# Masked attention and a gated convolution feed-forward on one core: the value product in two runs of six matmuls, and other places for the copies out of PSUM

## The chip, the cores and the metric

The kernel runs on one core of one Trainium2 chip. A core has a matrix engine (TensorE, PE in the profile, with its weight loads on a row of their own, PEld), VectorE (DVE), ScalarE (ACT), GpSimd (POOL) and SyncE (SP), which here issues nearly all DMAs. Each engine works through its own queue in the order of the program, and waits on semaphores where it needs another engine's result. TensorE writes only to PSUM, a small memory of eight banks, and VectorE or ScalarE must copy the results out. The metric is device time in microseconds of one execution.

## The reference, cut to what matters

```python
# q, k, v: (4, 8, 768, 64); proj: (64, 6)
q_bits = einsum(q, proj) > 0;  k_bits = einsum(k, proj) > 0      # six bits per row
mask   = bucket(q_bits)[:, None] == bucket(k_bits)[None, :]
scores = where(mask, q @ k.T / 8, -1e9)
attn   = exp(scores - max);  attn = attn / (sum(attn) + 1e-9)
x      = (attn @ v), heads side by side                           # (4, 768, 512)
gate   = sigmoid(causal 5-tap convolution of x, channel by channel)
out    = (gate * (x @ w_val)) @ w_out                             # (4, 768, 512)
```

## The kernel before, in words

There are 32 **units**, one for each batch and head. A unit has 768 queries, in six **tiles** of 128. A main loop goes over the 192 tiles of all units, and a pass `k` of it is called a **slot** here. The order of the work is written out by hand: the instructions stand on every engine in the order in which the Python code issues them, and generators (`moes`, `convs`, `preps`, `weights`, `ahead`, `avs`) are stepped at fixed places of a slot, each step issuing a piece of the work that lies beside attention.

Attention for tile `k` passes through several slots:

- `scores(k + 1)` (L266) issues the next tile's scores on TensorE: four matmuls into a PSUM tile `s`, of which there are two. So the scores of a tile need the buffer that the exponential of two tiles before has read.
- `maxima`, `factors`, `shifts` (L272 to L282) run on VectorE, then `exponentials` (L290) on ScalarE, with the row's sum from the accumulator. `row_sums` and `recip` run for two tiles at once, `normalise` (L305) on POOL.
- `transposes(k - 3)` (L314) turns the probabilities on TensorE, six 128 x 128 transposes into two PSUM tiles `tp`, of which there are two.
- `keep_transposed` (L323) copies both to `pt` in SBUF on ScalarE, at the start of the following slot. After a unit's last tile it appends the unit's value product to `avs`.
- `attn_v` (L337) is the value product: for each of six blocks of keys two matmuls, one for each half of the queries, which write the two halves of the partitions of one PSUM tile `av`. For the first three blocks both `pt` read are the first of their pair, for the others the second. The first half of the queries is tiles 0 to 2, the second is tiles 3 to 5. Every odd slot steps it twice, so that a unit's product comes as three **value runs** of four matmuls. After the last, two ScalarE copies (L345) take `av` to `x`.

A unit pair's `x` goes through `pair_x` (casts, five convolution taps, and after a batch's last pair the sigmoids), which appends the batch's feed-forward to `moes`. This consists of **chunks** of twelve matmuls into a PSUM tile of `ps_m`, which has one buffer: eight value chunks (`val`, 384 columns, L399) and six output chunks (`outp`, 512 columns, L424). A step of `moes` issues a third of a chunk, four matmuls. Behind the last, VectorE multiplies with the gate (L404), or ScalarE (VectorE near the gates) copies the output (L430, L432), which a DMA stores. `thin` leaves out the step in odd or even slots around the end of a batch. The last two output chunks of a batch wait in `hold` for the next batch's chunks, and then a whole chunk is issued in each of two slots. The last batch's feed-forward follows behind the loop.

In the first batch no chunk exists yet. Its slots share VectorE, ScalarE and POOL with the preparation of the weights, and carry the bit products (`bits` L204, `early_bits` L226), whose results VectorE marks (L207, L229).

## Time and profile before

| | us |
|---|---|
| runs: median, lowest, highest of 3 | 622.48, 621.9, 624.69 |
| profiled execution, first to last instruction (its span) | 620.8 |
| TensorE busy | 585.5 |
| VectorE busy | 437.6 |
| ScalarE busy | 421.4 |
| GpSimd busy | 395.6 |

The profiled execution's own time is its span, and the median of the runs lies 1.7 us above it. A row of a group or of the timeline names line, engine, operation, the tiles written and read and a count; numbers behind a bar are busy time and mean length, and then the idle time of the engine ahead of these instructions, with what ended it. A row of the busy times by stretch has the stretch, then for PE, PEld, DVE, ACT and POOL the busy time and the number of instructions, then TensorE's granted clock, the DMA share and GB/s. A matmul's length in the trace is modelled and overlaps the next one's, so what a block costs is read from its start to the next block's start.

### The profile page before, as it was taken

The page shows a single profiled execution, that of the slowest core. Times are in us where ns is not written, and L with a number is a line of the kernel's source. Part 1 is how long each engine was busy: PE and PEld are TensorE (multiplying, and loading weights), DVE is VectorE, ACT ScalarE, POOL GpSimd, SP SyncE. Part 2 cuts the span into 40 slices and gives each one's busy share as a digit, 9 for nine tenths or more (in the row PEclk, how much of TensorE's full clock was granted, in tenths as well). Part 3 has the DMA queues.
Part 4 walks back from the last instruction along what each step waited for, and adds up shares of the span by engine and source line. Part 5 has one row for each costly group of instructions (what it writes and reads, how often), then busy time and mean ns, then how long its engine had stood idle before and what let it go on. Part 6 is the DMA issues. An engine that isn't in the chain of part 4 may idle for free.

```text
span 620.8 us, 10648 instructions
## 1 busy us (share of the span) xinstructions
PE 585.5 (94%) x3496; PEld 423.4 (68%) x3496; DVE 437.6 (70%) x1017; ACT 421.4 (68%) x881; POOL 395.6 (64%) x373
## 2 busy tenths in 40 slices
PE   5789898989999999999999999999999999999997
PEld 2655565555657777776767777777667877775895
DVE  5869798998975866668575867569665877665532
ACT  2777777778778666777787676777787766765400
POOL 3576868778766765578564777568764777544321
PEclk9799999999999999999999999999999999999999
DMA  6467666564532235243433234333422213200111
GB/s 227 123 197 199 200 167 208 157 175 118 133 83 68 70 79 142 72 108 82 122 82 107 61 80 126 84 115 82 108 70 78 67 42 91 69 18 1 51 52 51
DMA packets 29031, 64.64 MB, mean 104 GB/s; under 512 B 4937, under 2 KB 10057, under 8 KB 28977
## 3 DMA queue, kind: packets, MB, share of 16 engines
q1 hardware_dynamic: 28832, 63.93, 37.8%
q8 instruction: 28, 0.46, 0.3%
q14 instruction: 27, 0.21, 0.1%
q10 hardware_dynamic: 144, 0.03, 0.0%
HBM read 30.60 MB, written 7.86 MB: 62 GB/s over the span
## 4 chain that ended last, share of the span: by engine, by line
PE 66%; DVE 12%; ACT 12%; DMA 5%; issue 3%; POOL 2%; SPq 1%; ACTq 0%; POOLq 0%; DVEq 0%
PE av L337 17%; PE s L266 16%; PE tp L314 12%; PE m L424 8%; PE m L399 7%; ACT p L290 5%; DVE nm L272 4%; ACT pt L323 3%; ACT x L345 2%; DMA w<-in_w_val_dram 2%; DVE g L368 2%; PE tp L399 1%; PE tp L424 1%; PE s L424 1%; DMA bk<-bq 1%
## 5 line engine op out<-in xcount | busy, mean ns | idle before, releaser
L305 POOL TENSOR_SCALAR p<-p,ri 128x768 f32<-128x768 f32 x192 | 210.5, 1100 | 156.0 <-DVE nb L282 130.8
L272 DVE TENSOR_REDUCE nm<-s 128x1 f32<-128x768 f32 x192 | 182.5, 950 | 61.2 <-PE s L266 61.0
L290 ACT ACTIVATE p<-s,nb,gs 128x768 f32<-128x768 f32 x192 | 192.6, 1003 | 46.2 <-DVE nb L282 41.9
L323 ACT COPY pt<-tp 128x384 f32<-128x384 f32 x384 | 165.7, 485 | 75.3 <-PE tp L314 74.4
L314 PEld LDWEIGHTS tp<-ident,p 128*128 128x128 f32 x1152 | 130.3, 142 | 72.2 <-issue 43.6
L314 PE MATMUL tp<-ident,p 128*128 128x128 f32 x1152 | 164.4, 279 | 2.6 <-ACT pt L323 2.1
L337 PE MATMUL av<-pt,vt 128*64 128x384 f32 x768 | 144.9, 498 | 0.0
L266 PE MATMUL s<-ak,aq 76*128 76x384 f32 x384 | 118.1, 389 | 23.2 <-ACT p L290 19.7
L266 PE MATMUL s<-bk,bq 128*128 128x384 f32 x384 | 101.3, 345 | 0.4 <-DVE bq L252 0.4
L337 PEld LDWEIGHTS av<-pt,vt 128*64 128x64 f32 x768 | 47.0, 136 | 61.5 <-issue 61.4
L266 PEld LDWEIGHTS s<-ak,aq 76*128 76x128 f32 x384 | 59.2, 194 | 38.7 <-ACT p L290 34.6
L368 DVE SCALAR_TENSOR_TENSOR g<-x,cw_sb,g 128x768 f32<-128x768 f32 x64 | 79.4, 1241 | 2.2 <-POOL g L366 2.1
L266 PEld LDWEIGHTS s<-bk,bq 128*128 128x128 f32 x384 | 71.7, 194 | 0.8 <-issue 0.8
L173 POOL TENSOR_TENSOR bq<-r,aq 128x768 fp32r<-128x768 f32 x31 | 59.2, 1909 | 0.1
L410 POOL TENSOR_TENSOR hl<-ht,hh 128x384 fp32r<-128x384 f32 x32 | 32.3, 1009 | 39.5 <-DVE hh L408 39.5
L345 ACT COPY x<-av 64x384 f32<-64x384 f32 x64 | 30.4, 475 | 29.7 <-PE av L337 29.0
L282 DVE TENSOR_SCALAR nb<-nm,gs 128x1 f32<-128x1 f32 x192 | 40.4, 211 | 3.5
L399 PE MATMUL m<-xh,wv 128*128 128x384 f32 x200 | 42.7, 337 | 0.0
L358 POOL TENSOR_TENSOR xl<-x,xh 128x384 fp32r<-128x384 f32 x32 | 33.4, 1059 | 13.8 <-DVE xh L357 13.8
L290 ACT ACTIVATION_READ_ACCUMULATOR p<-s,nb,gs 128x1 f32 x192 | 39.0, 203 | 0.0
L404 DVE TENSOR_TENSOR ht<-m,g 128x384 f32<-128x384 f32 x25 | 13.9, 556 | 35.6 <-PE m L399 29.2
L424 PE MATMUL m<-wo,hh 128*128 128x512 f32 x144 | 38.1, 394 | 0.0
(86 smaller groups left out, 486.9 us busy)
## 6 DMA issues: line engine op xcount, KB each, us to landing
r<-in_qk_dram SPq DMA_DIRECT2D x32, 384.0 KB
vt<-in_v_dram SPq DMA_DIRECT2D x16, 384.0 KB
out_dram<-o SPq DMA_DIRECT2D x24, 256.0 KB
ak<-aq SPq DMA_DIRECT2D x31, 192.0 KB
bk<-aq SPq DMA_DIRECT2D x31, 192.0 KB
bk<-bq SPq DMA_DIRECT2D x31, 192.0 KB
bq<-aq SPq DMA_DIRECT2D x31, 192.0 KB
hh<-in_qk_dram SPq DMA_DIRECT2D x16, 192.0 KB
```

What stands on the lines that cost most here:

```text
L173: nc.gpsimd.tensor_tensor(out=bq, in0=r, in1=aq.bitcast(FP32), op=ALU.subtract)
L266: nc.tensor.matmul(out=s[:, hf, 0:HS], lhsT=lq[0:n, qs], rhs=rk[0:n, hf * HS:(hf + 1) * HS], start=n == M, stop=n == P)
L272: nc.vector.tensor_reduce(out=nm, in_=s[:, :, 0:HS], axis=AX.XY, op=ALU.max, negate=True)
L290: nc.scalar.activation(out=p, in_=s[:, :, 0:HS], func=AF.Exp, bias=nb, scale=gs.pop(k), accum_out=sm[:, k % 2, 0:1])
L305: nc.gpsimd.tensor_scalar(out=p, in0=p, scalar1=rcs.pop(k), scalar2=1.0, op0=ALU.mult, op1=ALU.mult)
L314: nc.tensor.transpose(out=tp[:, n * P:(n + 1) * P], in_=p[:, kb * P:(kb + 1) * P], identity=ident)
L323: nc.scalar.copy(out=pt[:, :, qo:qo + P], in_=tp[:, 0:HS].rearrange("p (a b) -> p a b", b=P))
L337: nc.tensor.matmul(out=av[s * D:(s + 1) * D, 0:HS], lhsT=vt[:, kb, hh * D:(hh + 1) * D], rhs=pt[kb // 3][:, kb % 3, :], start=(kb == 0), s ...
L345: nc.scalar.copy(out=x[hh * D:(hh + 1) * D, o:o + HS], in_=av[s * D:(s + 1) * D, 0:HS])
L368: nc.vector.scalar_tensor_tensor(out=g, in0=x[:, k:k + S], scalar=w, in1=g, op0=ALU.mult, op1=ALU.add)
L399: nc.tensor.matmul(out=acc[:, 0:HS], lhsT=wv[wi][:, c, j * P:(j + 1) * P], rhs=xs_[(c, o)][xi], start=(m == 0), stop=(m == 11))
L424: nc.tensor.matmul(out=acc, lhsT=hs[(o, j)][hi][:, tb * P:(tb + 1) * P], rhs=wo[wi][:, j, :], start=(m == 0), stop=(m == 11))
```

## The change

- `attn_v` is stepped three times in every slot with `k % 3 == 2`, instead of twice in every odd one: two value runs of six matmuls for a unit. They stand behind the transposes, not ahead of them.
- `keep_transposed(k - 3)` follows `transposes(k - 3)` in its own slot. So a unit's value product begins in the slot in which its last tile is transposed (its *first run*; the *second run* comes three slots later).
- A step of `moes` issues half a chunk, six matmuls. It is called in two slots of three (`(1, 1, 0)[k % 3]`), not in every slot with thinner stretches; behind the gates twice in a slot instead of three times.
- What reads a PSUM tile of `av`, of a chunk or of the bits is put into a list, `readers`. The list is emptied by `read()`, which stands behind the exponential of a slot, and at the next request for an accumulator.
- `early_bits` steps at `k % 6` of 1 and 4 instead of 2 and 4, and the loop has one slot less.

```diff
@@ early_bits, bits @@
-            nc.vector.tensor_scalar(out=u[:, sl], in0=z[:, 0:HS], ...)
+            def mark(z=z, sl=sl):
+                nc.vector.tensor_scalar(out=u[:, sl], in0=z[:, 0:HS], ...)
+            soon(mark)
@@ attn_v @@
-        for s in range(2):
-            o = KW - 1 + s * HS
-            nc.scalar.copy(out=x[hh * D:(hh + 1) * D, o:o + HS], in_=av[s * D:(s + 1) * D, 0:HS])
...
+        def take():
...
+            for s in range(2):
+                o = KW - 1 + s * HS
+                nc.scalar.copy(out=x[hh * D:(hh + 1) * D, o:o + HS], in_=av[s * D:(s + 1) * D, 0:HS])
...
+        soon(take)
+
+    def soon(f):
+        readers.append(f)
+        if cur["end"]:
+            read()
+
+    def read():
+        while readers:
+            readers.pop(0)()
@@ acc_tile (and side_tile, prep) @@
+        read()
@@ val (outp alike, with store for gate) @@
-                if m:
-                    yield
                 for c in range(NP):
+                    if m == 6:
+                        later()
+                        yield
...
-            nc.vector.tensor_tensor(out=ht, in0=acc[:, 0:HS], in1=g[j][:, o:o + HS], op=ALU.mult)
+            def gate():
+                nc.vector.tensor_tensor(out=ht, in0=acc[:, 0:HS], in1=g[j][:, o:o + HS], op=ALU.mult)
+                todo.append(split)
...
+            soon(gate)
@@ main loop @@
-        for k in range(N + LAG + 1):
-            if 0 <= k - LAG - 1:
-                keep_transposed(k - LAG - 1)
+        for k in range(N + LAG):
...
                 exponentials(k)
+            read()
...
-            thin = k // 6 % 8 in (7, 0) and k < 186
-            for _ in range(3 if cur["gates"] else (1, 0)[k % 2] if thin else 1):
+            for _ in range(2 if cur["gates"] else (1, 1, 0)[k % 3]):
                 step(moes)
...
-            if 6 <= k < 60 and k % 6 in (2, 4):
+            if 6 <= k < 60 and k % 6 in (1, 4):
                 step(ahead)
-            if k % 2:
-                step(avs)
-                step(avs)
             if 0 <= k - LAG < N:
                 transposes(k - LAG)
+                keep_transposed(k - LAG)
+            if k % 3 == 2:
+                for _ in range(KB // 2):
+                    step(avs)
```

TensorE's queue before, in a slot with a value run between value chunks. `x2` and `x4` count instructions; `Activation` and `Pool` are the semaphores of ScalarE and POOL.

```order
L266 MATMUL s<-ak,aq 128x384 [waits Activation_49]
L266 MATMUL s<-ak,aq 128x384
L266 MATMUL s<-bk,bq 128x384 x2
L399 MATMUL m<-xl,wv_120 128x384 x4
L337 MATMUL av<-pt,vt 64x384 x4
L314 MATMUL tp<-ident,p 128x128 [waits Activation_49,Pool_49]
L314 MATMUL tp<-ident,p 128x128 x2
L314 MATMUL tp<-ident,p 128x128 [waits Activation_49]
L314 MATMUL tp<-ident,p 128x128 x2
```

The run stands ahead of the slot's transposes and this one waits for nothing. TensorE's queue after, in a slot with a unit's first run (scores are L274 now, transposes L322, the value product L345):

```order
L274 MATMUL s<-ak,aq 128x384 [waits Activation_49]
L274 MATMUL s<-ak,aq 128x384
L274 MATMUL s<-bk,bq 128x384 x2
L322 MATMUL tp<-ident,p 128x128 [waits Activation_49,Pool_49]
L322 MATMUL tp<-ident,p 128x128 x2
L322 MATMUL tp<-ident,p 128x128 [waits Activation_49]
L322 MATMUL tp<-ident,p 128x128 x2
L345 MATMUL av<-pt,vt 64x384
L345 MATMUL av<-pt,vt 64x384 [waits Activation_49]
L345 MATMUL av<-pt,vt 64x384 x4
```

The run has moved behind the transposes, no chunk stands in the slot, and the run's second matmul waits for ScalarE.

ScalarE's queue before, around a unit's copies of `av` to `x` (L345; L290 is the exponential, L323 the copies of transposes):

```order
L323 COPY pt<-tp 128x3x128 [waits PE_49,Activation_49]
L290 ACTIVATE p,sm<-s,nb,gs 128x768 [waits DVE_49,Pool_49]
L345 COPY x<-av 64x384 [waits PE_49]
L345 COPY x<-av 64x384
L323 COPY pt<-tp 128x3x128 [waits PE_49] x2
L290 ACTIVATE p,sm<-s,nb,gs 128x768 [waits DVE_49,Pool_49]
```

The copies of `av` stand ahead of the transposes' copies and of the next exponential. ScalarE's queue after, in two slots, the second with a first run and the store of an output chunk (L460; L298 is the exponential, L331 the copies of transposes):

```order
L298 ACTIVATE p,sm<-s,nb,gs 128x768 [waits DVE_49,Pool_49]
L331 COPY pt<-tp 128x3x128 [waits PE_49] x2
L298 ACTIVATE p,sm<-s,nb,gs 128x768 [waits DVE_49,Pool_49]
L460 COPY o<-m 128x512 [waits DMAHW7_49,DMAHW3_49]
L331 COPY pt<-tp 128x3x128 [waits PE_49] x2
```

Readers such as the store now follow the exponential, and the copies of the slot's own transposes come after both. A unit's copies of `av` take the place that the store has here, in the slot behind the unit's second run.

More of the change, by code (lines that the diff above doesn't have):

```diff
@@ L206, in bits @@
                                  tile_position=(0, 32 * jj))
-            nc.vector.tensor_scalar(out=u[:, sl], in0=z[:, 0:HS], scalar1=rows_sb[:, 0:1], scalar2=rows_sb[:, 1:2],
-                                    op0=ALU.is_ge, op1=ALU.mult)
+            def mark(z=z, sl=sl):
+                nc.vector.tensor_scalar(out=u[:, sl], in0=z[:, 0:HS], scalar1=rows_sb[:, 0:1], scalar2=rows_sb[:, 1:2],
+                                        op0=ALU.is_ge, op1=ALU.mult)
+            soon(mark)
         cur["u"] = u
@@ L223, in early_bits @@
                 yield
-                z = ps_m.tile([P, 512], FP32, name="m")
+                z = acc_tile()
                 for jj, t in enumerate(rows[hf]):
@@ L227, in early_bits, with keep @@
                                      tile_position=(0, 32 * jj))
-                t = hp.tile([P, HS], FP32, name="ht", bufs=2)
-                nc.vector.tensor_scalar(out=t.bitcast(FP32R), in0=z[:, 0:HS], scalar1=rows_sb[:, 0:1],
-                                        scalar2=rows_sb[:, 1:2], op0=ALU.is_ge, op1=ALU.mult)
-                nc.sync.dma_start(out=u[:, hf * HS:(hf + 1) * HS], in_=t)
+                def keep(z=z, u=u, hf=hf):
+                    t = hp.tile([P, HS], FP32, name="ht", bufs=2)
+                    nc.vector.tensor_scalar(out=t.bitcast(FP32R), in0=z[:, 0:HS], scalar1=rows_sb[:, 0:1],
+                                            scalar2=rows_sb[:, 1:2], op0=ALU.is_ge, op1=ALU.mult)
+                    nc.sync.dma_start(out=u[:, hf * HS:(hf + 1) * HS], in_=t)
+                soon(keep)
             early[i] = u
@@ L338, in attn_v @@
                                  start=(kb == 0), stop=(kb == KB - 1), tile_position=(0, s * D))
-        if hh == 0:
-            x = cur["x"] = xp.tile([P, S + KW - 1], FP32, name="x")
-            nc.gpsimd.memset(x[:, 0:KW - 1], 0.0)
-        x = cur["x"]
-        for s in range(2):
-            o = KW - 1 + s * HS
-            nc.scalar.copy(out=x[hh * D:(hh + 1) * D, o:o + HS], in_=av[s * D:(s + 1) * D, 0:HS])
-        if hh == 1:
-            if c == 0:
-                cur["xs"], cur["g"] = {}, []
-            convs.append(pair_x(b, c, x, cur["g"], cur["xs"]))
+        def take():
+            if hh == 0:
+                x = cur["x"] = xp.tile([P, S + KW - 1], FP32, name="x")
+                nc.gpsimd.memset(x[:, 0:KW - 1], 0.0)
+            x = cur["x"]
+            for s in range(2):
+                o = KW - 1 + s * HS
+                nc.scalar.copy(out=x[hh * D:(hh + 1) * D, o:o + HS], in_=av[s * D:(s + 1) * D, 0:HS])
+            if hh == 1:
+                if c == 0:
+                    cur["xs"], cur["g"] = {}, []
+                convs.append(pair_x(b, c, x, cur["g"], cur["xs"]))
+        soon(take)
[6 more added lines that the diff above has]
+            readers.pop(0)()
     def pair_x(b, c, x, gs, xs_):
@@ L376, in acc_tile @@
     def acc_tile():
+        read()
         pools = accs
@@ L401, in val @@
                     m += 1
-                later()
+            later()
             ht = hp.tile([P, HS], FP32, name="ht", bufs=2)
-            nc.vector.tensor_tensor(out=ht, in0=acc[:, 0:HS], in1=g[j][:, o:o + HS], op=ALU.mult)
+            def gate():
+                nc.vector.tensor_tensor(out=ht, in0=acc[:, 0:HS], in1=g[j][:, o:o + HS], op=ALU.mult)
+                todo.append(split)
             def split():
@@ L411, in split @@
                 hs[(o, j)] = (hh, hl)
-            todo.append(split)
+            soon(gate)
             yield
@@ L420, in outp @@
             for hi, wi in ((0, 0), (0, 1), (1, 0)):
-                if m:
-                    yield
                 for j in range(NP):
+                    if m == 6:
+                        later()
+                        yield
                     nc.tensor.matmul(out=acc, lhsT=hs[(o, j)][hi][:, tb * P:(tb + 1) * P],
@@ L426, in outp, with store @@
                     m += 1
-                later()
-            ob = op.tile([P, 512], FP32, name="o")
-            if cur["gates"]:
-                nc.vector.tensor_copy(out=ob, in_=acc)
-            else:
-                nc.scalar.copy(out=ob, in_=acc)
-            r0 = o + tb * P
-            nc.sync.dma_start(out=out[b, r0:r0 + P, :], in_=ob)
+            later()
+            def store():
+                ob = op.tile([P, 512], FP32, name="o")
+                if cur["gates"]:
+                    nc.vector.tensor_copy(out=ob, in_=acc)
+                else:
+                    nc.scalar.copy(out=ob, in_=acc)
+                r0 = o + tb * P
+                nc.sync.dma_start(out=out[b, r0:r0 + P, :], in_=ob)
+            soon(store)
             yield
@@ L512 @@
                 exponentials(k)
+            read()
             if k >= 60 or k % 2:
@@ L523 @@
             step(preps)
-            if 6 <= k < 60 and k % 6 in (2, 4):
+            if 6 <= k < 60 and k % 6 in (1, 4):
                 step(ahead)
-            if k % 2:
-                step(avs)
-                step(avs)
             if 0 <= k - LAG < N:
                 transposes(k - LAG)
+                keep_transposed(k - LAG)
+            if k % 3 == 2:
+                for _ in range(KB // 2):
+                    step(avs)
         accs[:] = [(ps_m, "m"), (ps_t, "tp"), (ps_s, "s"), (ps_t, "tp"), (ps_s, "s")]
         finish(avs)
+        read()
         cur["gates"] = 0
```

2 lines of the change are left out of this document (1 added, 1 removed).

## The prediction

> **What bounds the kernel now.** I read the page's first table, then the busy times by stretch, then TensorE's own timeline, where the distance from one start to the next shows what a block of matmuls really takes.
>
> ```profile
> span 620.8 us, 10648 instructions
> PE 585.5 (94%) x3496; PEld 423.4 (68%) x3496; DVE 437.6 (70%) x1017; ACT 421.4 (68%) x881; POOL 395.6 (64%) x373
> 35.00:187.50 152.50, 138.68 (x890) 87.19 (x886) 132.57 (x302) 114.72 (x248) 115.95 (x106) 1.00 0.58 162
> 187.50:331.10 143.60, 140.24 (x841) 104.05 (x841) 96.01 (x234) 108.87 (x225) 95.98 (x91) 1.00 0.36 92
> 331.10:471.70 140.60, 139.15 (x843) 103.85 (x841) 97.51 (x235) 104.09 (x219) 94.30 (x88) 1.00 0.35 92
> L272 DVE TENSOR_REDUCE nm<-s 128x1 f32<-128x768 f32 x56 | 53.1, 949 | 6.2 <-PE s L266 6.2
> ```
>
> The last row is the first stretch's own: 56 maxima in 152.5 us, so 2.72 us a slot, with VectorE busy for 132.57 of them. There VectorE is about as close to its limit as TensorE. From 187.5 on TensorE alone is full. One pair of slots there:
>
> ```profile
> 331.09 0.59 PE L266 MATMUL s<-ak,aq 76*128 76x384 f32 x2
> ...
> 331.88 0.86 PE L399 MATMUL m<-xh,wv 128*128 128x384 f32 x4
> 332.67 1.51 PE L337 MATMUL av<-pt,vt 128*64 128x384 f32 x8
> 334.11 0.88 PE L314 MATMUL tp<-ident,p 128*128 128x128 f32 x6
> 334.74 0.59 PE L266 MATMUL s<-ak,aq 76*128 76x384 f32 x2
> ...
> 335.53 0.86 PE L399 MATMUL m<-xh,wv 128*128 128x384 f32 x4
> 336.23 0.82 PE L314 MATMUL tp<-ident,p 128*128 128x128 f32 x6
> 336.80 0.43 PE L266 MATMUL s<-ak,aq 76*128 76x384 f32 x1
> ```
>
> Start to start, scores take 0.79, a third of a chunk 0.70, transposes 0.57 (0.63 after a value run). The slot with a value run takes 3.65, the one without 2.06: a run of four matmuls costs 1.59 (eight records, since each matmul leaves two).
>
> The next rows show what ScalarE does between two transposes, in a slot that has no chunk.
>
> ```profile
> 307.52 0.14 PEld L337 LDWEIGHTS av<-pt,vt 128*64 128x64 f32 x2 [0.18 <-issue]
> 307.84 0.14 PEld L337 LDWEIGHTS av<-pt,vt 128*64 128x64 f32 x2 [0.18 <-issue]
> 308.58 0.88 PE L314 MATMUL tp<-ident,p 128*128 128x128 f32 x6
> 309.17 0.86 ACT L323 COPY pt<-tp 128x384 f32<-128x384 f32 x2 [0.75 <-PE tp L314]
> 309.21 0.59 PE L266 MATMUL s<-ak,aq 76*128 76x384 f32 x2
> 309.92 1.01 ACT L290 ACTIVATE p<-s,nb,gs 128x768 f32<-128x768 f32 x1
> 310.01 0.82 PE L314 MATMUL tp<-ident,p 128*128 128x128 f32 x6
> 310.80 0.21 ACT L290 ACTIVATION_READ_ACCUMULATOR p<-s,nb,gs 128x1 f32 x1
> 310.90 0.49 ACT L323 COPY pt<-tp 128x384 f32<-128x384 f32 x1
> 311.07 0.45 PE L266 MATMUL s<-ak,aq 76*128 76x384 f32 x1 [0.24 <-ACT p L290]
> 311.39 0.22 DVE L282 TENSOR_SCALAR nb<-nm,gs 128x1 f32<-128x1 f32 x1
> 311.73 0.99 ACT L290 ACTIVATE p<-s,nb,gs 128x768 f32<-128x768 f32 x1
> 312.62 0.19 ACT L290 ACTIVATION_READ_ACCUMULATOR p<-s,nb,gs 128x1 f32 x1
> ```
>
> **The change, part by part.** Unless said otherwise, counts are for the loop from 187.5 us on: 21 units, TensorE-bound, so what TensorE saves or waits is the time.
>
> *Three value runs of a unit become two.* The weight loads at 307.52 and 307.84 show the step inside a run: 0.32 for a pair of records, 1.29 for four. So 0.30 of a run's 1.59 belongs to going in and out: the load waits for the matmuls ahead of it, and the transposes behind come 0.06 slower. After the change a run is entered from transposes and left into scores, which no row shows. Bounds are 0.20, if scores restart at once, and 0.30 as now; I take 0.25, between them. A unit pays 3 x 0.30 now and 2 x 0.25 then, 0.40 less: 21 x 0.40 = -8.4 (range -6.3 to -10.5). In "The mechanism", part 3 of "TensorE: Matmul & The Clock Gate", the Trainium skill says that a weight load overlaps running matmuls only if its row group differs. Both halves of the value product use the same rows, so by that rule each pair pays its own load and this term is 0; the trace disagrees, since the load at 307.52 runs under matmuls that are 0.32 apart.
>
> *Chunks in halves, not thirds.* 0.70 is four times the 0.175 of one matmul, and nothing is paid at its edges: 0. The end of the chunk has the same matmuls: 0.
>
> *Copies of `av` behind the exponential.* Now they stand before the transposes' copies and the next exponential:
>
> ```profile
> 217.64 0.87 PE L314 MATMUL tp<-ident,p 128*128 128x128 f32 x6
> 217.76 0.97 ACT L345 COPY x<-av 64x384 f32<-64x384 f32 x2 [0.48 <-PE av L337]
> 218.27 0.59 PE L266 MATMUL s<-ak,aq 76*128 76x384 f32 x2
> 219.50 1.01 ACT L290 ACTIVATE p<-s,nb,gs 128x768 f32<-128x768 f32 x1
> 220.65 0.44 PE L266 MATMUL s<-ak,aq 76*128 76x384 f32 x1
> 552.55 0.59 PE L266 MATMUL s<-ak,aq 76*128 76x384 f32 x2
> 554.93 0.44 PE L266 MATMUL s<-ak,aq 76*128 76x384 f32 x1
> 318.86 0.60 PE L266 MATMUL s<-ak,aq 76*128 76x384 f32 x2
> 321.23 0.44 PE L266 MATMUL s<-ak,aq 76*128 76x384 f32 x1 [0.43 <-ACT p L290]
> ```
>
> These slots take 2.38 instead of 2.06, since the scores wait for that exponential. The same happens once in each of 21 units, up to the slot at 552.55: 0.32 in 11 slots with a value chunk, 0.08 in 6 with the longer output chunk, 1.0 in 4 with no chunk (318.86 to 321.23 is 2.37 against 0.79 + 0.57). The sum is 8.0. In the new order the copies come when the exponential of their slot is done and the run has just ended, and 0.97 of copies ends well before the slot's transposes start (0.79 + 1.05 behind the run): -8.0 (at least -6, at most -8).
>
> *Slots without a chunk.* Scores issued at 309.21 are exponentiated by 312.81 (last rows above), and the scores two slots on use their buffer, 0.06 later (as 311.07 follows 311.01): any two slots in a row take 3.66. The run in every second slot covers that now, but four odd slots still lose 0.5 each to late copies (309.21 to 311.07 is 1.86 against 1.36): -2.0. After it, seven groups of three slots have no chunk (the two that `idle` takes and the rest of each hold), and in each, two short slots of 1.36 stand next to each other: 7 x (3.66 - 2.72) = +6.6 (range 5 to 9).
>
> *The value run behind its own slot's copies.* This is the term that decides. In a unit's first run, the second matmul reads a `pt` that the same slot's transposes and copy must fill first. ScalarE has in its queue: both copies of the slot before, the exponential, then this copy. From the transposes at 308.58 through 309.17 and 309.92 the copy comes at 310.90 and ends at 311.39. TensorE would be there earlier: transposes at 310.01, 0.57 for them and 0.10 of the run's 0.25 to enter (an estimate), 310.68; the second matmul starts at 311.39 + 0.06 = 311.45. So 0.77 of waiting, in every first run, whatever chunk stood before it, because all is counted from the transposes of the slot before. Of 21 first runs 16 pay 0.77, two behind a whole chunk 0.4, three in a slot without a chunk 0.66: 12.3 + 0.8 + 2.0 = +15.1. If 0.32 of what the first matmul does alone meanwhile is not lost, 0.45 remains and the sum is 9; if the exponential itself is late by 0.3, it is 21. I take 15, which the rows give directly.
>
> *Readers a slot later.* Five of these first runs have the store of an output chunk between exponential and copy:
>
> ```profile
> L432 ACT COPY o<-m 128x512 f32<-128x512 f32 x12 | 7.0, 587 | 3.2 <-PE m L424 2.2
> DVE ht L404 <- PE m L399: 29.2, 18, 3.0
> DVE ht L229 <- PE m L226: 4.2, 6, 1.3
> ```
>
> 5 x about 0.5 = +2.3 (0 to 2.9). VectorE's 29.2 of waiting for a chunk goes, but VectorE has 47 of 143.6 us free there: 0. The accumulator is read in the slot that has no chunk, before the next chunk's start: 0 (up to +2). `split` on POOL comes later, and its results are needed chunks later: 0. The output's DMAs leave SP a slot later, with nothing queued behind that is short of time: 0.
>
> *The first stretch.* The two-run form needs per three slots 3.66 for the two short ones and 0.79 + 0.57 + 1.94 + 0.25 = 3.55 for the long one, 7.2, and 7.9 with the wait: 7.5 on average, 141 for the 56 slots that take 152.5 now. But VectorE's 132.6 of work stay; only waits like the 4.2 above go. Bounds: -12, if it reaches these 141; +8, if maxima that come in twos behind other VectorE work are late. I take 0. `early_bits` keeps its eight groups. Start and tail have the same work, and one slot less has none in it: 0.
>
> Sum: -8.4 - 8.0 - 2.0 + 6.6 + 15.1 + 2.3 + 0 = +5.6. The profiled span of 620.8 becomes 626.4. The median of the runs, 622.48, is 1.7 above that span: 628.1, or 628.
>
> **Rivals.**
> - *The first stretch shortens* (faster). If VectorE's waits there were what delayed maxima, 152.5 goes towards 141: -12 + 5.6, 616. It decides from -8.6 on, 2.57 a slot. For it: 16 copies and marks no longer stop VectorE. Against: 87% busy and in order.
> - *The wait is only 0.45* (no change): 15.1 becomes 9, sum -0.5, 622. For it: two halves of the array that work apart. Against: the second half's three matmuls remain in either case, 1.94.
> - *The first stretch lengthens* (slower, 634 or more). Short slots in twos give VectorE no slack between maxima.
> - *Fewer runs save nothing*: 628 + 8.4 = 636. The rows with steps of 0.32 speak against it. The rule of "TensorE: Matmul & The Clock Gate" that is weighed above, from the Trainium skill, would give it.
> - *The change has no effect*, 622: excluded almost by the order, in which runs and copies do move.
>
> **Numbers.** Forecast 0.40, of which 0.06 falls within 0.5%; shorter first stretch 0.22; half wait 0.23; longer first stretch 0.10; no saving 0.03; no effect 0.02. A measurement tells about 0.5%, 3.1 us. Slower 0.34 + 0.10 + 0.03 = 0.47, same 0.06 + 0.23 + 0.02 = 0.31, faster 0.22. The forecast's own range is 624 to 632. The whole range goes to 613 (the first stretch at -12 and the wait a little cheaper) and 636.
>
> **What would show it.** Right: about 63 value runs of twelve records; slots with a first run some 0.8 longer than with a second; a wait of `av` for the copies of `pt` in the list of waits, near 20 us in all; no slot stretched by the copies of `x`. Wrong: no such wait, or a first stretch that differs from 152 us by more than 5.

## The result and the profile after

The changed kernel takes 660.83 us (median of 4 runs, 658.62 to 662.1) against 622.61 for the kernel before in the same session: 1.0605 times as long, with an interval of 1.0577 to 1.0632. The direction was forecast, the size was not: 628 us, with a range to 636. In the runs below, one execution of four of e12, e13 and e14 was slow at a lower granted clock, and their times are medians of the other three.

The head of the page after, and the busy times of both kernels by stretch. The stretches are cut at the starts of the 63rd and of the 187th of the 190 blocks of scores that each trace shows apart, so that both kernels have the same work in each: the first stretch, the loop behind it, and the tail. Columns are the stretch and its length, then busy time and instructions of PE, PEld, DVE, ACT and POOL, the granted clock, the DMA share and GB/s. Before:

```profile
35.00:181.90 146.90, 133.31 (x855) 83.93 (x851) 127.04 (x290) 111.01 (x240) 114.10 (x105) 1.00 0.60 167
181.90:548.90 367.00, 361.80 (x2187) 269.71 (x2185) 252.31 (x608) 270.36 (x566) 240.38 (x226) 1.00 0.33 86
548.90:620.80 71.90, 66.65 (x355) 53.21 (x353) 33.02 (x61) 21.06 (x41) 24.06 (x24) 0.99 0.09 34
```

After:

```profile
span 656.8 us, 10644 instructions
PE 600.8 (91%) x3496; PEld 440.2 (67%) x3496; DVE 449.7 (68%) x1014; ACT 419.8 (64%) x884; POOL 391.3 (60%) x373
35.00:197.20 162.20, 143.15 (x861) 91.01 (x860) 137.63 (x295) 112.71 (x241) 119.20 (x105) 0.98 0.54 148
197.20:587.20 390.00, 370.83 (x2192) 282.29 (x2191) 257.35 (x602) 267.62 (x566) 231.38 (x226) 1.00 0.31 80
587.20:656.80 69.60, 63.77 (x336) 51.50 (x334) 30.08 (x58) 20.55 (x40) 23.66 (x24) 0.99 0.09 34
```

So the first stretch is 15.3 us longer, the loop 23.0, the tail 2.3 shorter: +36.0. ScalarE and GpSimd are no busier, VectorE is busier by 12.1 (10.6 of them in its row sums, see the last section), and no engine is full. The time went into waits of TensorE. Its busy time hides part of them, since a matmul's end is modelled, so they are counted from start to start: for every pair of neighbouring blocks (scores then transposes, transposes then scores, and so on) what each takes over the nearly shortest of its kind in the same kernel. In us, first stretch / loop:

| kernel | length | scores late behind transposes | transposes late behind scores | scores late behind a run | all waits |
|---|---|---|---|---|---|
| before | 146.9 / 367.0 | 20.3 / 13.5 | 0.8 / 1.4 | 0 / 0 | 22.7 / 16.5 |
| after | 162.2 / 390.0 | 16.7 / 11.8 | 5.7 / 10.1 | 11.8 / 14.9 | 37.0 / 39.8 |

What is not wait, 350.5 us in the loop before, is 350.2 after. The list of waits after (waiting engine and line, what it waited for, us in all, times, longest) has three waits, two of them on both of TensorE's rows, that the kernel before lacks or has far smaller:

```profile
DVE xh L377 <- ACT x L355: 29.2, 12, 8.7
PEld av L345 <- ACT pt L331: 21.1, 22, 2.1
PEld tp L322 <- POOL p L313: 14.7, 18, 1.4
PE av L345 <- ACT pt L331: 8.5, 11, 1.4
PE tp L322 <- POOL p L313: 7.8, 11, 1.1
```

The value product waits for the copies of its own slot, as forecast. Transposes wait for GpSimd's normalise, which was not. And VectorE waits 29.2 us for the copies of `av`; the row of that wait before:

```profile
DVE xh L357 <- ACT x L345: 10.6, 5, 6.3
```

*A first run and a second run.* The timeline after, a slot with a second run (from 375.30) and one with a first run (from 383.67), which reads a `pt` of its own slot:

```profile
375.30 0.82 PE L322 MATMUL tp<-ident,p 128*128 128x128 f32 x6
376.04 2.16 PE L345 MATMUL av<-pt,vt 128*64 128x384 f32 x12
378.13 0.62 PE L274 MATMUL s<-ak,aq 76*128 76x384 f32 x2
...
383.67 1.01 ACT L298 ACTIVATE p<-s,nb,gs 128x768 f32<-128x768 f32 x1
383.76 0.82 PE L322 MATMUL tp<-ident,p 128*128 128x128 f32 x6
384.51 2.83 PE L345 MATMUL av<-pt,vt 128*64 128x384 f32 x12
384.65 0.87 ACT L331 COPY pt<-tp 128x384 f32<-128x384 f32 x2
385.19 0.20 PEld L345 LDWEIGHTS av<-pt,vt 128*64 128x64 f32 x4 [0.49 <-ACT pt L331]
387.27 0.30 PEld L274 LDWEIGHTS s<-ak,aq 76*128 76x128 f32 x2 [0.60 <-issue]
```

The second run takes 376.04 to 378.13, 2.09. The first starts at 384.51, its second matmul gets weights only at 385.19, behind the copy that began at 384.65, and it lasts to 387.27: 2.76. The wait is 0.67 in a slot where nothing else is late.

*A late normalise.* The other new wait has more steps. Rows of the timeline after, around the copies of `av` to `x` (L435 is `split`'s subtraction, `hl`):

```profile
357.76 0.17 DVE L308 RECIPROCAL ri<-s 128x2 f32<-128x2 f32 x1
359.33 0.62 PE L274 MATMUL s<-ak,aq 76*128 76x384 f32 x2
359.44 0.97 ACT L355 COPY x<-av 64x384 f32<-64x384 f32 x2 [0.18 <-PE av L345]
359.78 0.51 PE L274 MATMUL s<-bk,bq 128*128 128x384 f32 x2
359.95 1.68 DVE L377 CAST xh<-x 128x384 fp32r<-128x384 f32 x2 [1.86 <-ACT x L355]
360.40 1.01 POOL L378 TENSOR_TENSOR xl<-x,xh 128x384 fp32r<-128x384 f32 x1 [1.39 <-DVE xh L377]
361.70 1.06 POOL L378 TENSOR_TENSOR xl<-x,xh 128x384 fp32r<-128x384 f32 x1 [0.29 <-DVE xh L377]
361.82 0.94 DVE L280 TENSOR_REDUCE nm<-s 128x1 f32<-128x768 f32 x1
362.73 1.01 POOL L435 TENSOR_TENSOR hl<-ht,hh 128x384 fp32r<-128x384 f32 x1
363.70 1.82 POOL L173 TENSOR_TENSOR bq<-r,aq 128x768 fp32r<-128x768 f32 x1
364.41 1.14 DVE L304 TENSOR_SCALAR s<-sm 128x2 f32<-128x2 f32 x1 [0.35 <-ACT p L298]
365.50 1.78 POOL L313 TENSOR_SCALAR p<-p,ri 128x768 f32<-128x768 f32 x2
366.46 0.87 PE L322 MATMUL tp<-ident,p 128*128 128x128 f32 x6 [1.06 <-POOL p L313]
```

The scores of the second row are complete by 360.29, but their maxima begin at 361.82: they stand on VectorE's queue behind the two casts, and these wait 1.86 for ScalarE's copies. GpSimd waits too: its first `xl` stands idle 1.39 for the first cast. Then `xl`, `xl`, `hl` and `bq` follow each other almost without a gap until 365.52, and only there comes the normalise, at 365.50, though its reciprocal was done at 357.93. TensorE's transposes wait 1.06 for it. So not the late row sums at 364.41 hold these transposes up, but GpSimd's queue. The same holds at all ten places of the loop where transposes come more than 0.25 late (9.4 of the 10.1 us): each time the normalise starts as `bq` ends, long after its reciprocal, and at nine of the ten an `xl` stands ahead of that `bq`.

VectorE's wait for `x` comes at every unit pair: 1.3 to 2.2 us ahead of the first cast, eleven times in the loop, with the short waits between the casts 22.0 in all. Before, the copies were issued at the end of one slot and the casts in the next. The change's `read()` issues the copies, and `step(convs)` stands on the next line: both now come in one slot. In "Tensor Engine Instruction (MATMUL, LD_WEIGHTS)" of "Perfetto Trace Analysis" the Trainium skill says that VectorE, ScalarE and GpSimd take their queues strictly in order. The trace agrees, with 1.5 us of maxima that were ready and did not start.

### The profile page after: what moved, and what is told of

It is laid out like the page before. It is cut to its first block, busy times and chain, and to the rows that moved or that the text cites. A ratio compares the mean times of both kernels' runs of the same rounds, so it can differ in the third digit from the quotient of the medians.

```text
span 656.8 us, 10644 instructions
## 1 busy us (share of the span) xinstructions
PE 600.8 (91%) x3496; PEld 440.2 (67%) x3496; DVE 449.7 (68%) x1014; ACT 419.8 (64%) x884; POOL 391.3 (60%) x373
## 4 chain that ended last, share of the span: by engine, by line
PE 62%; DVE 17%; ACT 12%; POOL 6%; issue 2%; DMA 1%; ACTq 0%; DVEq 0%; POOLq 0%
PE av L345 19%; PE s L274 15%; PE tp L322 11%; PE m L421 6%; DVE nm L280 6%; ACT p L298 5%; PE m L450 5%; POOL bq L173 2%; DVE g L388 2%; ACT pt L331 2%; POOL p L313 1%; DVE xh L377 1%; POOL hl L435 1%; PE tp L421 1%; PE tp L450 1%
## 5 line engine op out<-in xcount | busy, mean ns | idle before, releaser
L313 POOL TENSOR_SCALAR p<-p,ri 128x768 f32<-128x768 f32 x192 | 205.8, 1079 | 187.2 <-DVE nb L290 184.9
L331 ACT COPY pt<-tp 128x384 f32<-128x384 f32 x384 | 165.9, 485 | 122.8 <-PE tp L322 122.1
L298 ACT ACTIVATE p<-s,nb,gs 128x768 f32<-128x768 f32 x192 | 192.2, 1001 | 64.3 <-DVE nb L290 58.3
L322 PE MATMUL tp<-ident,p 128*128 128x128 f32 x1152 | 161.3, 277 | 11.5 <-POOL p L313 7.8
L345 PE MATMUL av<-pt,vt 128*64 128x384 f32 x768 | 157.3, 497 | 8.7 <-ACT pt L331 8.5
L322 PEld LDWEIGHTS tp<-ident,p 128*128 128x128 f32 x1152 | 136.1, 142 | 37.7 <-POOL p L313 14.7
L274 PE MATMUL s<-ak,aq 76*128 76x384 f32 x384 | 119.3, 392 | 26.0 <-ACT p L298 24.3
L274 PEld LDWEIGHTS s<-ak,aq 76*128 76x128 f32 x384 | 59.1, 193 | 74.8 <-ACT p L298 39.7
L345 PEld LDWEIGHTS av<-pt,vt 128*64 128x64 f32 x768 | 56.9, 137 | 77.7 <-issue 54.8
L274 PE MATMUL s<-bk,bq 128*128 128x384 f32 x384 | 101.0, 344 | 0.4 <-DVE bq L260 0.4
L388 DVE SCALAR_TENSOR_TENSOR g<-x,cw_sb,g 128x768 f32<-128x768 f32 x64 | 81.3, 1271 | 7.8 <-POOL g L386 7.5
L274 PEld LDWEIGHTS s<-bk,bq 128*128 128x128 f32 x384 | 71.9, 194 | 0.8 <-issue 0.8
L435 POOL TENSOR_TENSOR hl<-ht,hh 128x384 fp32r<-128x384 f32 x32 | 32.3, 1010 | 35.5 <-DVE hh L433 35.5
L377 DVE CAST xh<-x 128x384 fp32r<-128x384 f32 x32 | 23.2, 733 | 30.8 <-ACT x L355 29.2
L290 DVE TENSOR_SCALAR nb<-nm,gs 128x1 f32<-128x1 f32 x192 | 40.6, 212 | 3.5
L298 ACT ACTIVATION_READ_ACCUMULATOR p<-s,nb,gs 128x1 f32 x192 | 38.7, 202 | 0.0
L421 PEld LDWEIGHTS m<-xh,wv 128*128 128x128 f32 x200 | 35.4, 188 | 0.6 <-DVE ht L428 0.5
```

What stands on the lines that cost most here:

```text
L274: nc.tensor.matmul(out=s[:, hf, 0:HS], lhsT=lq[0:n, qs], rhs=rk[0:n, hf * HS:(hf + 1) * HS], start=n == M, stop=n == P)
L290: nc.vector.tensor_scalar(out=nbs[k], in0=nms.pop(k), scalar1=gs[k], scalar2=None, op0=ALU.mult)
L298: nc.scalar.activation(out=p, in_=s[:, :, 0:HS], func=AF.Exp, bias=nb, scale=gs.pop(k), accum_out=sm[:, k % 2, 0:1])
L313: nc.gpsimd.tensor_scalar(out=p, in0=p, scalar1=rcs.pop(k), scalar2=1.0, op0=ALU.mult, op1=ALU.mult)
L322: nc.tensor.transpose(out=tp[:, n * P:(n + 1) * P], in_=p[:, kb * P:(kb + 1) * P], identity=ident)
L331: nc.scalar.copy(out=pt[:, :, qo:qo + P], in_=tp[:, 0:HS].rearrange("p (a b) -> p a b", b=P))
```

## The experiments

Times are medians of 4 runs in each case (e18: 10; e12, e13 and e14: 3), ratios are to the kernel before on the same chip, with 95% intervals. The medians of the kernel before in these sessions were 621.6 to 622.95.

| run | us | ratio |
|---|---|---|
| e1_copy_first | 647.98 | 1.0399 [1.0368, 1.0431] |
| e2_run_later | 662.91 | 1.0651 [1.0601, 1.0701] |
| e3_sums_last | 664.03 | 1.0662 [1.0632, 1.0692] |
| e4_readers_now | 666.64 | 1.0698 [1.0671, 1.0724] |
| e5_bq_later | 679.24 | 1.0933 [1.0859, 1.1007] |
| e6_before_bq_later | 695.78 | 1.1205 [1.1165, 1.1245] |
| e7_both | 678.56 | 1.0913 [1.0888, 1.0937] |
| e8_before_readers | 644.04 | 1.0377 [1.0341, 1.0413] |
| e9_before_runs_of_six | 634.27 | 1.0195 [1.0159, 1.0231] |
| e10_before_half_chunks | 639.23 | 1.0269 [1.0238, 1.0299] |
| e11_before_both | 631.59 | 1.0142 [1.011, 1.0175] |
| e12_run_later_x_later | 629.75 | 1.0116 [1.0094, 1.0137] |
| e13_run_later_av_now | 629.42 | 1.0119 [1.0069, 1.017] |
| e14_both_x_later | 627.36 | 1.0079 [1.0058, 1.01] |
| e15_change_x_later | 646.66 | 1.0387 [1.037, 1.0403] |
| e16_copy_first_x_later | 630.66 | 1.0133 [1.0092, 1.0174] |
| e17_mixed | 614.57 | 0.9873 [0.9831, 0.9915] |
| e18_before_x_later | 622.85 | 1.0004 [0.9985, 1.0022] |

### The run's wait for its own slot's copies

e1, the change with a slot's transposes and copies ahead of its exponential where a first run follows:

```diff
                 scores(k + 1)
+            if 0 <= k - LAG < N and k % 6 == 2:
+                transposes(k - LAG)
+                keep_transposed(k - LAG)
             if k < N:
                 exponentials(k)
...
-            if 0 <= k - LAG < N:
+            if 0 <= k - LAG < N and k % 6 != 2:
```

> The changed kernel, but in the slot of a unit's first value run the transposes' copies stand ahead of that slot's exponential on ScalarE. Theory W (TensorE waits in the first run for a copy that stands behind an exponential, which itself waits for VectorE; 27.1 us of stretched runs in the changed kernel's trace): the copy comes about 0.9 us after its transposes begin, 0.3 to 0.4 of the wait stays in each of 31 runs, about 11 in all, so 16 less: 645. Theory P (GpSimd's normalise is late, so that the transposes of these slots wait; 15.8 us of such waits against 2.2 before): these stay, and the exponential now waits with them, 655 to 662. Theory G (two short slots next to each other, bound by the two score buffers): no change, 661.

Measured 647.98, 12.9 less than the change. Scores late behind a run fall from 26.7 to 11.5 us, but transposes late behind scores rise from 15.8 to 24.2: the wait is real, and part of what it hid comes out.

e2, the change with every value run one slot later and ahead of the transposes, so that its `pt` were copied a slot before:

```diff
-            for _ in range(2 if cur["gates"] else (1, 1, 0)[k % 3]):
+            for _ in range(2 if cur["gates"] else (0, 1, 1)[k % 3]):
                 step(moes)
...
+            if k % 3 == 0:
+                for _ in range(KB // 2):
+                    step(avs)
             if 0 <= k - LAG < N:
                 transposes(k - LAG)
                 keep_transposed(k - LAG)
-            if k % 3 == 2:
-                for _ in range(KB // 2):
-                    step(avs)
```

> The changed kernel, but value runs stand in every slot with k % 3 == 0, one slot after the unit's last copies, and ahead of that slot's transposes; half chunks stand in the other two slots. Theory W: the 27.1 us of waiting in the runs go, 634. Theories W and P together: the transposes of the long slot also come 2.1 us later, so GpSimd's lateness is covered there, 13 more: 621. Theory G: short slots still stand in twos, so little changes, 655 to 661.

Measured 662.91, no gain. No run waits for its copies now, but scores late behind transposes have grown to 24.5 / 30.9. In the loop, a loss of 1.2 to 2.6 us comes once in twelve slots, once for each unit pair. Rows of e2's timeline at one:

```profile
363.46 0.59 PE L274 MATMUL s<-ak,aq 76*128 76x384 f32 x2
363.89 0.52 PE L274 MATMUL s<-bk,bq 128*128 128x384 f32 x2
364.17 1.00 ACT L298 ACTIVATE p<-s,nb,gs 128x768 f32<-128x768 f32 x1
365.28 0.97 ACT L355 COPY x<-av 64x384 f32<-64x384 f32 x2
365.79 1.67 DVE L377 CAST xh<-x 128x384 fp32r<-128x384 f32 x2 [3.54 <-ACT x L355]
366.23 1.01 POOL L378 TENSOR_TENSOR xl<-x,xh 128x384 fp32r<-128x384 f32 x1 [2.81 <-DVE xh L377]
367.65 0.94 DVE L280 TENSOR_REDUCE nm<-s 128x1 f32<-128x768 f32 x1
369.13 0.99 ACT L298 ACTIVATE p<-s,nb,gs 128x768 f32<-128x768 f32 x1 [1.99 <-DVE nb L290]
370.26 0.62 PE L274 MATMUL s<-ak,aq 76*128 76x384 f32 x2 [1.76 <-ACT p L298]
```

Scores issued at 363.46 are complete by 364.41. VectorE stands idle for 3.54 us in front of the casts (1.86 in the change), which wait for copies that ScalarE begins at 365.28, behind an exponential. The maxima of those scores start at 367.65, 3.2 late, the exponential at 369.13, and TensorE, which needs its buffer, waits 1.76 us. That gave theory X below.

### Other guesses for the late normalise

e3, the change with the row sums behind the shift on VectorE:

```diff
-            if pair:
-                row_sums(k - 2)
             if k < N:
                 factors(k)
+                shifts(k)
             if pair:
+                row_sums(k - 2)
                 recip(k - 2)
             if 0 <= k - 2 < N:
                 normalise(k - 2)
-            if k < N:
-                shifts(k)
```

> The changed kernel, but the sums of rows and their reciprocal stand behind the shift on VectorE, so they no longer delay the exponential. In the changed kernel the sums of two columns take 0.16 us alone, but 0.87 to 1.15 in 11 of 96 cases beside GpSimd's subtraction; 28.5 us in all against 17.9 before. Theory V (these delays reach the exponential and through it the copies): 10 us less, 651. Rival: the exponential gains 0.4 but the normalise comes 0.4 later, which with theory P costs as much: 658 to 665.

664.03, not faster. Transposes are later behind scores by 2.4 in the first stretch and 0.7 in the loop, and scores behind a run by 1.0 and 2.5; whether the later normalise does it was not taken apart.

e5 to e7 begin a unit's operand `bq` on GpSimd two slots later (two more `yield` in `prep`): e5 on the change, e6 on the kernel before, e7 on e1.

> The changed kernel, but GpSimd's subtraction for the next unit (bq, 1.9 us, and the DMAs behind it) stands two slots later. In the changed kernel's trace all of bq, both xl of a pair (1.0 each) and often an hl (1.0) stand in the same slot (k % 12 == 6), in the kernel before they stood apart (bq at 0 and 6, xl at 8). Theory B (GpSimd's work is bunched in one slot, so that a normalise comes late for transposes and VectorE's small operations take longer beside it): most of the 15.8 us of waits of transposes go, and a few of the waits in the runs, 643 to 649. Theory W alone (only the copy behind the exponential): no change, 658 to 663.

> The kernel before, with the same edit: bq two slots later, which there puts it into the slot of the pair's xl (k % 12 == 8). Theory B: the bunch of the changed kernel is made in the kernel before, 11 pairs at 1.2 us or more and something in the first batch, 632 to 640. Rival (the place of bq is harmless, the transposes there stand behind a chunk or a run that covers it): 621 to 625.

> The changed kernel with both edits: the first run's copies ahead of the exponential, and bq two slots later. Theories W and B together: of 648 with the first edit alone, the 24 us of waits of transposes for normalise go but for 3, 627 to 632. If the two were the same wait seen twice: 643 to 648.

679.24, 695.78 and 678.56. The edit brought a cost of its own, so these say little: in all three the next unit's scores wait for the DMAs that follow `bq` (10.9 us in e5, 23.4 in e6). In e5's loop the transposes' lateness did halve, from 10.1 to 5.0, as GpSimd's queue above would have it.

### The parts of the change on the kernel before

e4 and e8 take the deferral by itself: e4 is the change with `soon(f)` calling `f()` at once, e8 the kernel before with `soon`, `read` and the readers of the change.

> The changed kernel, but each reader of PSUM (copies of av, gate, store, marks) is issued at once and not a slot later. The prediction's step: the deferral is worth the 8 us that the copies of av cost in the loop before, so without it 669. Rival: in the new order the copies of av delay the next exponential by about 1 us in a slot that is long anyway, and the first runs no longer have a store ahead of the copy (5 x 0.5): within 3 of 661.

> The kernel before, with the deferred readers alone (copies of av, gate, store and marks follow the exponential of the next slot). The prediction's step: the copies of av no longer delay an exponential, 8 us less, 614. Rival (theory B: the deferral moves the casts of x and the split of a chunk towards the slot of bq, or the stretch of the copies was only the sign of a wait that has other causes): 620 to 628.

e4 is 5.8 slower than the change, e8 22.2 slower than the kernel before. In the change's order the run ends a slot, so that copies issued at once would stand on ScalarE ahead of the next exponential while the run still goes: in e4's trace they begin at 385.47, and the exponential, whose operand is ready at 385.45, follows at 386.46. There the deferral helps a little. On the kernel before, I had expected a gain. VectorE's wait for `x` rises there from 10.6 to 41.9 us, and the loop from 367.0 to 390.7, of which 14.7 is chunks that wait for the one accumulator buffer. Its first stretch, though, is 3.5 shorter.

e9 to e11 take the runs and the chunks, with readers at once:

```diff
e9:
-            if k % 2:
-                step(avs)
-                step(avs)
+            if k % 3 == 0:
+                for _ in range(KB // 2):
+                    step(avs)
e10 (val and outp yield at m == 6):
+            for _ in range(2 if cur["gates"] else (1, 1, 0)[k % 3]):
                 step(moes)
e11: both, with (0, 1, 1)[k % 3]
```

> The kernel before, with one edit: a unit's value product comes in two runs of six matmuls in the slots with k % 3 == 0 (before: three runs of four in odd slots), still ahead of the slot's transposes. Chunks, copies and readers stay. Theory A (the two runs of six are worth their saved entries and exits, about 0.36 us for each of 32 runs less, and cost nothing where nothing is moved with them): 608 to 614 with the 11.5 us of entries, at least clearly below 622. Theory B (slots with a run of six and a third of a chunk, 2.1 + 0.7 us, are too long and the slots without too short for the exponential chain, so that the short ones wait): 622 to 632, with waits of TensorE in scores or transposes of the slots without a run.

> The kernel before, with one edit: chunks of the feed-forward in halves of six matmuls, in slots with k % 3 of 0 and 1, none in k % 3 == 2; two halves a slot behind the gates. Value runs of four in odd slots, copies and readers as before. Theory A (chunks in halves cost nothing by themselves; the loss of the change comes from the copies behind the exponential and from the deferred readers): 618 to 626. Theory B (uneven slots make the exponential chain late: slots with a half chunk and a run of 4 have 1.05 + 1.4, those without any only scores and transposes): 630 to 650, with waits of transposes and scores in the slots without a chunk.

> The kernel before, with both edits: two runs of six in slots with k % 3 == 0, half chunks in the other two slots of three. The readers are immediate; it differs from the change with its run a slot later (measured 662.9) by the deferred readers alone, and by the place of the early bits. Theory A (deferral of the readers is what makes that kernel slow): 610 to 620. Theory B (the even split into slots of about equal length is itself what exposes every late exponential, since no slot is longer than the chain): 645 to 662.

All three are slower: +12.7, +17.6 and +10.0. In e9 TensorE's work apart from waits does fall, by 1.8 us in the first stretch and 2.9 in the loop, but waits grow by 8.6 and 6.6. In e10 the loop loses 14.8: its slots with neither chunk nor run make scores and transposes late by some 15 more, as its second theory had it. In e11 the pieces fit together again (run in one slot of three, half chunks in the other two) and the loop is at 369.9 with 22.3 of waits. e11 and e2 hold nearly the same order, e2 with the readers deferred, and lie 31 us apart. That is the price of the deferral there. e11 itself lies between its two theories: the even split alone doesn't make the loss, but the deferral isn't all of it either.

### Theory X: casts that wait for deferred copies hold up the maxima

Four runs. e12 is e2 with `pair_x` starting two slots later from the second batch on, e13 is e2 with the copies of `av` alone issued at once (gates, stores and marks stay deferred), e14 is the control, e11 with e12's delay, and e15 is the change itself with that delay.

```diff
e12, e14, e15:
     def pair_x(b, c, x, gs, xs_):
+        if b:
+            yield
+            yield
e13:
-        soon(take)
+        take()
```

> The change with its run a slot later (e2, 662.9), with one more edit: from the second batch on, what follows a unit pair's x (casts, taps) begins two slots later. Theory X (the deferred copies of av stand behind an exponential, and the casts of the same slot, which wait for them on VectorE, hold up the maxima behind them; that wait was 51.2 us over the kernel in e2 and 17.9 in e11): the loop behind the first batch falls from 394 towards the 370 of e11, so 638 to 646 in all, and the wait of xh for x falls to under 20 us. Theory Y (the copies' own place on ScalarE, or the other deferred readers, cost the time): 655 to 665.

> The change with its run a slot later (e2, 662.9), with one more edit: the copies of av are issued at once behind the last run, not deferred; gates, stores and bits stay deferred. Theory X (the copies of av together with the casts that follow them are the cost of the deferral): 630 to 638, as e11 with all readers at once (631.6). Theory Y (the deferred gates, stores and marks are): 650 to 663.

> e11 (the kernel before with both splits, readers at once, 631.6) with casts and taps two slots later from the second batch on. It shows what that delay is worth where the copies of av aren't deferred. Theory X: 626 to 632, since only 17.9 us of VectorE's wait for x is there to be saved and most of it costs nothing. Rival (the delay spreads VectorE's and GpSimd's work and is a gain by itself, which would feign theory X in the run with deferral): 610 to 622.

> The change itself with casts and taps two slots later from the second batch on. Theory X: the loop behind the first batch loses the lateness that the casts bring, 645 to 654. Theory Y (first runs that wait for the copies of their own slot are the loss by themselves, 14.9 us in the loop): 657 to 664.

e12 falls from 662.91 to 629.75, below the range that theory X gave, and e13 to 629.42, near e11's 631.59. Either way of parting copies and casts takes back the whole deferral. The delay without the deferral is worth 4.2 (e14). From the list of waits, e2 and then e12:

```profile
DVE xh L377 <- ACT x L355: 51.2, 16, 6.7
PE s L274 <- ACT p L298: 42.0, 56, 2.4
```

```profile
DVE xh L380 <- ACT x L355: 8.0, 5, 3.7
PE s L274 <- ACT p L298: 25.0, 45, 2.4
```

And rows of e12's timeline, at the copies and the casts of a unit pair:

```profile
354.12 0.97 ACT L355 COPY x<-av 64x384 f32<-64x384 f32 x2
354.69 0.59 PE L274 MATMUL s<-ak,aq 76*128 76x384 f32 x2
355.68 0.96 DVE L280 TENSOR_REDUCE nm<-s 128x1 f32<-128x768 f32 x1 [1.00 <-PE s L274]
357.45 0.62 DVE L380 CAST xh<-x 128x384 fp32r<-128x384 f32 x2
```

The copies are as late as ever, but the maxima at 355.68 follow their scores, and the casts find `x` ready. The loop is 363.6 us long, 3.4 shorter than in the kernel before. The change itself gains 14.2 by the delay (e15: loop 376.5; VectorE's waits for `x` in the loop 22.0 to 0, transposes late behind scores 10.1 to 3.7, scores late behind transposes 11.8 to 6.9, scores late behind a run hardly changed, 14.9 to 15.8). So in the change rather more of the loss comes by way of GpSimd, whose `xl` waits for the casts (6.4 of transposes' lateness), than by the maxima of theory X (4.9 of scores' lateness).

### Whether the two costs add, and a faster version

e16 is e1 with the delay. e17 has deferred readers throughout, three runs of four in the first 60 slots as before, and e12's order and delay behind them. e18 is the kernel before with the delay alone.

```diff
e17, against e12:
-            if k % 3 == 0:
-                for _ in range(KB // 2):
-                    step(avs)
+            for _ in range(2 * (k % 2) if k < 60 else KB // 2 * (k % 3 == 0)):
+                step(avs)
...
-            if 6 <= k < 60 and k % 6 in (1, 4):
+            if 6 <= k < 60 and k % 6 in (2, 4):
```

> e1 (the change with transposes and copies of the first run's slot ahead of its exponential, 648.0) with casts and taps two slots later from the second batch on. If the run's wait for its own slot's copies (-12.9 by e1) and the casts that wait for the deferred copies of av (-14.2 by e15) are two costs beside each other: 633 to 638. If they are one lateness seen twice: 644 to 649.

> Deferred readers throughout; in the first 60 slots three runs of four in odd slots as before; from slot 60 on two runs of six in slots with k % 3 == 0, ahead of the transposes, half chunks in the other slots, and casts two slots later from the second batch on. From the stretches of earlier runs: the first stretch of e8 (ends at 178.4), the loop of e12 (363.6) and its tail (69.6) make 611.6 in the profile. Theory X and the stretches being independent: 609 to 616, faster than before. Rival (the stretches depend on each other, a late first batch is caught up later): 617 to 626.

> The kernel before with casts and taps two slots later from the second batch on, nothing else. Control for e17: what the delay alone is worth there. VectorE waits 10.6 us for x in the kernel before, most of it where it costs nothing: 619 to 623. Rival (the delay alone is the gain): 612 to 617.

e16 is 630.66: from 660.8, the copies first alone give -12.9, the delay alone -14.2, both -30.2, 3.1 more than the sum. They are two costs. The loop of e16 has the length of the kernel before, 367.0, and its first stretch is 156.2 against 146.9; that, and a tail 1.4 shorter, is what is left.

e17 takes 614.57, 1.3% less than the kernel before (0.9831 to 0.9915). Its stretches:

```profile
35.00:178.80 143.80, 133.88 (x848) 85.25 (x846) 128.69 (x288) 110.11 (x238) 114.31 (x105) 1.00 0.60 166
178.80:542.70 363.90, 356.32 (x2185) 272.38 (x2185) 246.15 (x605) 268.10 (x568) 236.83 (x226) 1.00 0.33 86
542.70:612.30 69.60, 65.26 (x354) 54.21 (x352) 31.29 (x58) 21.31 (x42) 23.73 (x24) 0.99 0.10 36
```

143.8, 363.9 and 69.6 are those of e8 and e12 that it was put together from (143.4, 363.6, 69.6). The delay alone gives nothing on the kernel before (e18), so the 8 us come from the two runs of six, the half chunks and the deferral, once the casts are out of the way and the first stretch keeps its runs of four. What each of the three gives was not taken apart.

## Why the prediction was wrong

The sum was +5.6 and came out at +36.0. By its own steps:

- **Copies of `av` behind the exponential, -8.0: the step that failed.** It followed the copies on ScalarE and left out who reads `x`. The casts are issued in the same slot and wait on VectorE for the copies; the next maxima stand behind them there, and on GpSimd `xl` waits for the casts and a normalise stands behind `xl` and `bq`. Copies and casts in one slot cost 14.2 in the change (e15), and about 30 on e11's order (e2 against e11, e12 and e13). What the step counted is real: with the casts later (e15), the loop's slots no longer lose the 0.3 that the copies took before. But in the change the term of -8 came out as a loss. The forecast that no slot would be stretched by the copies of `x` failed with it: they stretch slots by way of VectorE and GpSimd.
- **The value run behind its own slot's copies, +15.1, and the stores, +2.3: the mechanism right for the loop, left out for the first stretch.** Scores late behind a run are 14.9 in the loop, over 20 first runs. Six lose 0.67, where 0.77 was worked out; six lose only 0.30, since their transposes came late themselves; two lose 0.47; four with a store of an output chunk ahead of the copy lose 0.96 to 1.17, so up to 0.50 for the store; and two lose 1.82, where the sigmoids of a batch and a table load of 1.28 delay ScalarE. That the sum comes near is luck in part. The rival with 0.45 is refuted by the clean runs. But the first stretch has the same first runs, and there the term was put at 0 because VectorE was thought to set the pace. It lost 11.8. The wait of `av` for `pt`, forecast near 20, is 21.1 on the weight loads.
- **The first stretch, 0 between -12 and +8: the second step that failed, +15.3 and out of its bounds.** Waits of TensorE grew by 14.3 there, 11.8 of them behind first runs: VectorE's pace did not cover them. The rival that it lengthens had been given 0.10. Two runs of six alone lengthen it by 6.8 (e9), copies first takes 7.3 off the change (e1: 154.9), and with three runs of four it is 143.8 (e17). Why runs of six cost there also in e9's order, where no run waits for its own slot's copies, was not taken apart.
- **Three runs to two, -8.4: mis-sized.** The transposes ahead of a run take 0.74 instead of 0.57 (375.30 to 376.04), six pairs at 0.32 take 1.93 of the 2.09, and the scores behind take 0.81 instead of 0.79 in the slots without a wait: 0.35 for a run, not 0.25. Two of them against three at 0.30 save 0.20 a unit, 4 us in the loop; all that isn't wait fell by 0.3 in the change and by 2.9 in e9. Where the saving is seen it is under half the term, and in e9 the waits take more than it gives.
- **Chunks in halves, 0: right** for the change (a half value chunk takes 1.05, six times 0.175). The halves alone on the kernel before cost 17.6 (e10), because every sixth slot then has neither a chunk nor a run, and the losses come there. The change puts its runs into the slots without a half chunk.
- **Slots without a chunk, -2.0 and +6.6: the second right in size.** The loop after has seven such pairs of short slots. Five lose 0.90 to 0.92 between transposes and scores, where 0.94 was worked out; the other two lose 2.1 and 2.4, and 0.90 and 0.91 once the casts are later (e15). The -2.0 can't be told from the -8.0 in these runs: with both and the pairs together, scores late behind transposes would fall by 3.4, and they fell by 1.7 in the change and by 6.6 in e15.
- **Not foreseen:** normalise that comes late for the transposes, +8.7 in the loop. It is GpSimd's queue, with `xl` late behind the casts and `bq` behind `xl`, and goes with the delay of the casts (10.1 to 3.7).

With the casts later the loop is 9.5 longer than before (e15), against the +5.6 worked out. What is left over then is the first stretch.

## What to carry to other kernels

When an instruction is issued later, follow its result: a reader issued in the same pass now waits at the head of its own in-order queue, and holds up whatever stands behind it, here the maxima of the next tile on VectorE and, one engine further, a normalise on GpSimd. Try the parts of a change one at a time and together, stretch by stretch: here runs of six (+13), half chunks (+18) and deferral (+22) each lost on the kernel before, and together, with the casts two slots later and the first batch left as it was, they gained 8 us. A wait that vanishes without a gain (e2) can give way to another with a cause of its own: look for the engine that idles in front of a ready instruction.

## What the runs showed of the hardware

Some VectorE instructions from SBUF to SBUF become much longer when they start beside a running GpSimd instruction, and end just after it. The row sums of 128 x 2 numbers, 0.16 alone, took 1.14 at 364.41, and ended at 365.55, 0.03 after the `bq` that ran from 363.70 to 365.52; at 382.43, beside a normalise that reads one tensor, they took 0.73. In e2 the two casts, 0.62 together in e12, took 1.67 beside an `xl`. Not all do so: beside the same instructions `factors` and `shifts`, of 128 x 1, stay at 0.15 and 0.21 in the trace after, and the maxima, which read PSUM, at 0.95. Before and after, the groups of the row sums (count, busy us, mean ns):

```profile
L296 DVE TENSOR_SCALAR s<-sm 128x2 f32<-128x2 f32 x96 | 17.9, 186 | 6.7 <-ACT p L290 6.2
```

```profile
L304 DVE TENSOR_SCALAR s<-sm 128x2 f32<-128x2 f32 x96 | 28.5, 297 | 9.9 <-ACT p L298 9.9
```

In "SBUF: two separate sides" of "SBUF — State Buffer" the Trainium skill says that GpSimd and VectorE, the latter in certain modes only, take a shared pair of ports as an exclusive lock: who starts first holds it for the whole instruction, and the other blocks. The trace agrees: the short instruction ends when the long one does. So where a 0.16 us instruction lands beside GpSimd's work decides whether it takes 0.16 or 1.1, and a reordering moves that. No run here shows what these longer row sums cost in all; e3, which takes them out of the exponential's way, is not faster.
